# Moving the second exp, the weight sums and the casts of one unit in a fused attention and bilinear kernel

## The chip, the cores and the metric

The kernel runs on one core of a Trainium2 chip. A core has five engines with a queue each: TensorE (PE, matrix products), VectorE (DVE), ScalarE (ACT), GpSimd (POOL) and SyncE (SP), which here only issues transfers. The metric is the time of one execution on the device in microseconds (us), the median of several.

## What is computed

Chunked attention in chunks of 64 tokens, with its heads put side by side to 4608 tokens of 512 features, and behind it a bilinear layer of width 1536:

```python
batch, n_heads, seq, head_dim = (8, 8, 576, 64)
q_c = q.reshape(B, H, nc, chunk, D)            # chunk = 64, k_c and v_c likewise
scores = scale * np.matmul(q_c, k_c.transpose(0, 1, 2, 4, 3))
...
attn = np.exp(scores)
attn = attn / (np.sum(attn, axis=-1, keepdims=True) + 1e-09)
out = np.matmul(attn, v_c)
...
x = np.ascontiguousarray(attn_out.transpose(0, 2, 1, 3)).reshape(B * S, H * D)
a = x @ w_a
b = x @ w_b
return (a * b @ w_out).astype(np.float32)
```

The inputs and the output are float32 in the chip's memory. Inside, the attention is in bfloat16 and the bilinear layer in float16, with sums in PSUM in float32.

## The kernel before

**Tiling.** Attention goes in 18 units of 256 tokens, the bilinear layer in 9 blocks of 512 tokens, two units each. A unit is loaded (`load`, L181 and L193), cast to bfloat16 (`cast`, L212, mostly on POOL), transposed (units 0 to 4 on TensorE with copies on DVE and ACT, `transpose_pe`, L226 and L234; later ones by a transposing transfer, `transpose_dma`, L239), and then goes through `scores` (32 products, L257, and two exps on ACT, L266), `sums` (products with ones, L273, and logs, L283), `inverse` (exp of the negative log, L292) and `values` (32 products, L306, and two products with the inverse on DVE, L315, which make `xT`). `bring(U)` casts q and k of unit U, loads q of the next, transposes, casts v (`bring_v`) and loads k and v of the next.

**The bilinear layer.** Block 0 (`ab_step`, 12 steps `ft`) and block 1 (the same in 24 half steps, 256 tokens at a time: first the 12 steps for unit 2's tokens, then the 12 for unit 3's) use plain products: `x @ w_b` into PSUM (L368), a copy to SBUF by ACT (L376), `x @ w_a` and DVE's product of both (L377), which is `ab`. In half steps the PSUM banks alternate, pa and pq for `w_b`, pc and po for `w_a`. From block 2 on a form with seven products in place of eight is used (a Strassen variant). It needs sums of quarters of the weights (`combine_w`, L134, DVE: three parts and a fourth for each of six column pairs), of the tokens (`combine_x`, L398, DVE), of `w_out` (`combine_wo`, L163, POOL) and of `ab` (`combine_ab`, L498, POOL, four parts for each of three row pairs j). Its products are p1 to p7 of a `Group` (L418): p1 makes A, ACT copies A into B (L436), p6 adds to B, ACT copies that out as `u` (L429), p2 finishes A (`b_sb`), p5 adds to B and ACT copies it out as `v` (`v_sb`), p7 makes C. In the next step DVE adds v and u to C (`add7`, L456 and L457), p3 finishes B, p4 finishes C, and DVE multiplies (L468).

**The output product.** Block 0 uses `out_part` (L622, 12 products for each of four tiles in three parts) and a copy by ACT (L613). Later blocks use `OutGroup` (L554), also with seven products, which are dealt out in chunks of six matmuls between the products of the next block's steps (`chunks`).

**Order.** Nothing reorders the work: every engine runs its instructions in the order in which the program writes them. `at` puts the attention of the next block into fixed places (K, i, n) of the steps. In block 1 the order is written out by hand: `h(n)` does the next n half steps, and between them stand the scores, sums and values of units 3 to 5, `bring` of units 6 and 7 and block 0's output tiles. `combo()` writes the next of 18 weight sums. PSUM banks come from named pools of one bank each (pt has two, pb is two pools in turn), SBUF tiles from pools of fixed numbers of buffers.

Of the kernel before, what the change touches and what calls it, by code (L numbers as in the profile page):

```python
# [16 lines left out]
def kernel(  # L17
# [10 lines left out]
    nc = tc.nc  # L28
# [125 lines left out]
    def combine_wo(part, j):  # L154
        k = slice(2 * j, 2 * j + 2)
        k2 = slice(HFT + 2 * j, HFT + 2 * j + 2)
        b11, b12 = wo_sb[:, k, 0:256], wo_sb[:, k, 256:512]
        b21, b22 = wo_sb[:, k2, 0:256], wo_sb[:, k2, 256:512]
        t1, t2, t3, t4 = [t[:, k] for t in wo_t]
        o, x0, x1, op = (  # L160
            (t3, b22, b12, SUB), (t2, t3, b11, ADD), (t4, b21, t2, SUB), (t1, b12, b11, SUB)
        )[part]
        nc.gpsimd.tensor_tensor(out=o, in0=x0, in1=x1, op=op)  # L163
# [53 lines left out]
    def transpose_pe(U, names="qk"):  # L217
        if U not in qkt:
            qkt[U] = qkt_pool.tile([128, 2, 2, NKT, 128], BF16, name="qkt")
        for n in names:  # L220
            w = "qk".index(n)
            src = raw.pop((n, U))
            tp = bank().bitcast(BF16).rearrange("c (i m p) -> c i m p", i=2, m=NKT)
            for i in range(2):
                for m in range(NKT):
                    nc.tensor.transpose(  # L226
                        tp[:, i, m, :],
                        src[:, i, 2 * m:2 * m + 2, :].rearrange("p j d -> p (j d)"),
                        identity,
                    )  # L230
            dst = qkt[U][:, w].rearrange("c g m (p i) -> c i m g p", i=2)
            for i in range(2):
                cp = nc.vector.tensor_copy if w == 0 or U == 1 else nc.scalar.copy
                cp(out=dst[:, i], in_=tp[:, i].rearrange("c m (g p) -> c m g p", g=2))  # L234
# [10 lines left out]
    E_of = {}  # L245
    ln_of = {}
    rs_of = {}

    def scores(U, pools=(None, None)):
        t = qkt.pop(U)  # L250
        E_of[U] = sm_pool.tile([128, 2, NKT, 2, 64], BF16, name="E")
        sc = [bank(p).rearrange("p (m g s) -> p m g s", m=NKT, g=2) for p in pools]
        for m in range(NKT):
            for g in range(2):
                for j in range(2):
                    for cl in range(2):
                        nc.tensor.matmul(  # L257
                            sc[j][cl * 64:cl * 64 + 64, m, g, :],
                            t[j * 64:j * 64 + 64, 1, g, m, cl * 64:cl * 64 + 64],
                            t[j * 64:j * 64 + 64, 0, g, m, cl * 64:cl * 64 + 64],  # L260
                            start=m == 0 and g == 0,
                            stop=True,
                            skip_group_check=True,
                        )
        for j in range(2):
            nc.scalar.activation(out=E_of[U][:, j], in_=sc[j], func=AF.Exp, scale=scale)  # L266

    def sums(U, halves=None):
        E = E_of[U]
# [19 lines left out]
    def inverse(U, cl=None):  # L289

        for c in [slice(0, 2)] if cl is None else [cl]:
            nc.scalar.activation(  # L292
                out=rs_of[U][:, c], in_=ln_of[U][:, c], func=AF.Exp, scale=-1.0
            )

    def values(U):
        E, rs, vr = E_of.pop(U), rs_of.pop(U), raw.pop(("v", U))
        K, u = divmod(U, 2)
        if u == 0:
            x_tiles[K] = x_pool.tile([128, NKT, BLK], FP16, name="xT")  # L300
        av = [bank().rearrange("p (m g s) -> p m g s", m=NKT, g=2) for _ in range(2)]
        for m in range(NKT):
            for g in range(2):
                for cl in range(2):
                    for j in range(2):
                        nc.tensor.matmul(  # L306
                            av[cl][j * 64:j * 64 + 64, m, g, :],
                            vr[cl * 64:cl * 64 + 64, g, 2 * m + j, :],
                            E[cl * 64:cl * 64 + 64, j, m, g, :],
                            start=True,  # L310
                            stop=True,
                        )
        for cl in range(2):
            x = x_tiles[K][:, :, 256 * u:256 * u + 256]
            nc.vector.tensor_tensor(  # L315
                out=x.rearrange("p m (g c s) -> p m g c s", g=2, c=2)[:, :, :, cl, :],
                in0=av[cl],
                in1=rs[:, cl].rearrange("p m (g s) -> p m g s", g=2),
                op=MULT,
            )  # L320
# [13 lines left out]
    def bring(U, before_v=()):  # L334

        if U >= NU:
            return
        cast(U, "qk")
        load(U + 1, "q")
        transpose_dma(U)  # L340
        for args in before_v:
            cast(*args)
        bring_v(U)
# [288 lines left out]
    with tc.manual_schedule(  # L632
# [64 lines left out]

        for ft in range(NFT):
            ab_step(0, ft)
            if 3 <= ft < 10:  # L700
                combo()
            if ft == 6:
                transpose_pe(2)
            if ft == 8:
                slot(2)
            if ft == 9:
                sums(2)
                inverse(2)
            if ft == 10:
                values(2)  # L710

        cast(4, "qk")
        bring(5, [(4, "v")])

# [2 lines left out]
        def chunk(n=1):  # L717
            for _ in range(min(n, len(outs))):
                outs.pop(0)()

        def half(ft, u):
            ab_step(1, ft, 256 * u, 256 * u + 256)
            if ft > 9 if u == 0 else ft != 5 and ft != 9 and ft != 11:
                combo()
            if u == 1 and ft in (3, 5, 7):
                combine_w(ft // 2 - 1, 3)
            if u == 1 and ft % 2 and ft > 6:
                for part in range(3):
                    combine_ab(1, part, ft // 2 - 3)

# [2 lines left out]
        def h(n=1):  # L733
            for _ in range(n):
                half(*halves.pop(0))

        def normalize(U):
            sums(U)
            inverse(U)

        def out_0(tg):
            for p in range(3):
                out_part(0, tg, p, psum_b)
# [5 lines left out]
        h(3)  # L749
        scores(3)  # L750
        h(3)
        normalize(3)
        h(2)
        values(3)
        bring(6)
        h(8)
# [6 lines left out]
        normalize(4)  # L763
        h(1)
        scores(5)
        bring(7)
        h(1)
        values(4)
        h(1)
        spread[:] = [psum_q, psum_o]  # L770
        normalize(5)
        out_0(2)
        spread[:] = [psum_t]
        values(5)
        h(1)
        combine_x(2, (0, 1))
        whole = bank(psum_q)
        nc.tensor.matmul(whole, warm_in[:, :128], warm_in, start=True, stop=True)
        out_0(3)
        assert not halves and not combos  # L780

        attention = {}
# [29 lines left out]
        def attend(K, i, n):  # L812
# [2 lines left out]

        last = None
        chunks = {
            2: (0, 1, 1, 1, 1, 2, 1, 2, 1, 1, 2, 1),
            4: (1, 1, 1, 1, 2, 1, 1, 2, 2, 0, 1, 1),
            NBLK - 1: (1,) * 12,  # L820
        }
# [7 lines left out]

        for K in range(2, NBLK):  # L830
            for i in range(NWP):
                if K == 2 and i == 0:
                    for j in range(3):
                        combine_wo(3, j)
                if i == (2 if K == 2 else 1):
                    for j in range(3):
                        combine_ab(K - 1, 3, j)
                if i == 1:
                    bring(2 * K + 4)
                elif i == 3 and K > 2:  # L840
                    bring(2 * K + 5)
                elif i == 3:
                    cast(9, "qk")
                    load(10, "q")
                    transpose_dma(9)
                if i == 0:
                    g = OutGroup(K - 1)
                    outs += [
                        lambda g=g, n=n, th=th: g.part(n, th) for n in range(7) for th in range(2)
                    ]  # L850
                now = Group(K, i)
                now.p1()
                if last:
                    last.add7()
                chunk(chunks.get(K, chunks[4])[2 * i])
                if last:
                    last.p3()
                attend(K, i, 0)
                now.p6()
                if last:  # L860
                    last.p4()
                    finish(last)
                if K == 2 and i < 3:
                    combine_w(i + 3, 3)
                if K == 2 and i == 4:
                    bring_v(9)
                now.p2()
                chunk(chunks.get(K, chunks[4])[2 * i + 1])
                attend(K, i, 1)
                now.p5()  # L870
                now.p7()
                last = now
        ends = [
# [46 lines left out]
```

## Time and profile before

| | us |
|---|---|
| median of 5 runs | 309.06 |
| lowest and highest | 307.19, 311.4 |
| the profiled execution | 311.4 |
| its span, first to last instruction | 309.6 |

The profile is that of one execution; each of its views counts from the span's start. Its page says how busy each engine is and which chain of work ended last. TensorE's granted clock is full speed in all 40 slices. The 40 slices of the span, 7.7 us each, show TensorE's busy tenths, and the share of the 16 transfer engines, high up to about 108 us:

```profile
PE   2879999999997999998999999999999999999995
...
DMA  7999999999999999488929953995392001100025
```

How to read it: a line of the timeline has start and length in us, engine, line of the kernel, operation, what is written from what, shapes, and in brackets the idle time of the engine just before with what ended it. PE's rows overlap, since matmuls are pipelined; a stall is best read from the distance of starts: a matmul of 256 columns follows the last after 0.109 us, one of 512 after 0.217.

### The profile page before, as it was taken

The numbers are of one execution on the slowest core, as the hardware profiler recorded it, in microseconds if no ns is written. First come the engines' busy times: TensorE is split into PE (matmuls) and PEld (weight loads), VectorE is DVE, ScalarE is ACT, GpSimd is POOL, SyncE is SP. The second block draws the span as 40 slices with busy tenths as digits, with TensorE's granted clock in tenths as the row PEclk, the third lists the DMA queues.
The fourth block names the chain that finished last, engine by engine and source line by source line (L and its number), as shares of the span: only waits on it lengthen the run. The fifth ranks groups of instructions, "written<-read, shape, count | busy, mean of one in ns | idle before, by whom it ended". The sixth has DMA issues, their size and how long they took to land.

```text
span 309.6 us, 8537 instructions
## 1 busy us (share of the span) xinstructions
PE 291.5 (94%) x3497; PEld 231.6 (75%) x3499; DVE 213.1 (69%) x339; ACT 195.7 (63%) x353; POOL 192.7 (62%) x180
## 2 busy tenths in 40 slices
PE   2879999999997999998999999999999999999995
PEld 1534467765586888887888888888888888888884
DVE  3455673995757497578856885787678677965772
ACT  1643567348485658676768686768675877566531
POOL 0565758993859978915892588268727811780560
PEclk9999999999999999999999999999999999999999
DMA  7999999999999999488929953995392001100025
GB/s 229 307 382 265 265 314 338 214 208 203 211 245 248 201 206 281 81 201 185 257 57 238 234 162 70 209 263 146 78 227 97 11 2 70 51 20 2 1 80 193
DMA packets 143079, 54.56 MB, mean 176 GB/s; under 512 B 120256, under 2 KB 137152, under 8 KB 143040
## 3 DMA queue, kind: packets, MB, share of 16 engines
q1 hardware_dynamic: 142896, 53.88, 69.4%
q8 instruction: 27, 0.44, 0.6%
q10 hardware_dynamic: 144, 0.13, 0.1%
q14 instruction: 12, 0.10, 0.1%
HBM read 37.75 MB, written 9.44 MB: 152 GB/s over the span
## 4 chain that ended last, share of the span: by engine, by line
PE 59%; DMA 17%; POOL 9%; SPq 6%; DVE 5%; ACT 2%; issue 1%; POOLq 0%; DVEq 0%
PE pb L418 15%; PE pc L418 11%; PE pa L418 10%; PE po L554 10%; PE pq L554 9%; DMA st<-in_moe_w_a_dram 5%; DMA st<-in_v_dram 5%; SPq L181 4%; DMA st<-in_moe_w_out_dram 3%; POOL wot L163 2%; DMA st<-in_moe_w_b_dram 2%; POOL so L498 2%; DMA st<-in_k_dram 2%; SPq L193 2%; ACT E L266 1%
## 5 line engine op out<-in xcount | busy, mean ns | idle before, releaser
L418 PEld LDWEIGHTS <-t 128*128 128x128 f16 x504 | 48.3, 98 | 11.6 <-issue 5.9
L498 POOL TENSOR_TENSOR so<-ab_sb 128x512 f16<-128x512 f16 x23 | 26.5, 1154 | 45.2 <-DVE ab_sb L468 45.2
L456 DVE TENSOR_TENSOR c_sb<-pc,v_sb 128x512 f32<-128x512 f32 x42 | 29.0, 689 | 32.6 <-ACT v_sb L429 31.5
L418 PE MATMUL pb<-s,wa 128*128 128x256 f16 x336 | 50.6, 273 | 0.0
L418 PE MATMUL pa<-xT,wb 128*128 128x256 f16 x336 | 50.4, 273 | 0.0
L554 PEld LDWEIGHTS <-ab_sb 128*128 128x128 f16 x384 | 37.6, 98 | 4.7 <-issue 0.4
L418 PEld LDWEIGHTS <-wb 128*128 128x128 f16 x336 | 32.9, 98 | 4.0
L429 ACT COPY u_sb<-pb 128x512 f32<-128x512 f32 x42 | 24.7, 588 | 16.8 <-PE pb L418 11.6
L418 PEld LDWEIGHTS <-wa 128*128 128x128 f16 x336 | 31.7, 98 | 4.3 <-issue 0.2
L212 POOL CAST k_raw<-st 128x1024 bf16<-128x1024 f32 x17 | 18.2, 1068 | 26.3 <-DMA st<-in_k_dram 26.3
L468 DVE SCALAR_TENSOR_TENSOR ab_sb<-pb,b_sb 128x512 f16<-128x512 f32 x42 | 28.9, 688 | 7.6 <-PE pb L418 7.0
L468 DVE SCALAR_TENSOR_TENSOR ab_sb<-pc,c_sb 128x512 f16<-128x512 f32 x42 | 28.9, 688 | 5.6 <-PE pc L418 4.7
L554 PEld LDWEIGHTS <-so 128*128 128x128 f16 x288 | 28.0, 98 | 5.7 <-issue 1.2
L429 ACT COPY b_sb<-pa 128x512 f32<-128x512 f32 x42 | 25.0, 595 | 8.5 <-PE pa L418 7.3
L436 ACT COPY pb<-pa 128x512 f32<-128x512 f32 x42 | 24.5, 583 | 9.0 <-PE pa L418 9.0
L457 DVE TENSOR_TENSOR pc<-pc,u_sb 128x512 f32<-128x512 f32 x42 | 29.0, 689 | 0.0
L212 POOL CAST v_raw<-st 128x1024 bf16<-128x1024 f32 x18 | 19.2, 1064 | 14.7 <-DMA st<-in_v_dram 5.8
L498 POOL TENSOR_TENSOR so<-so,ab_sb 128x512 f16<-128x512 f16 x23 | 26.7, 1160 | 1.8
L429 ACT COPY v_sb<-pb 128x512 f32<-128x512 f32 x42 | 24.7, 587 | 4.8 <-PE pb L418 4.7
L498 POOL TENSOR_TENSOR ab_sb<-ab_sb 128x512 f16<-128x512 f16 x23 | 26.9, 1169 | 0.0
L418 PE MATMUL pc<-s,t 128*128 128x256 f16 x168 | 25.2, 272 | 1.1 <-DVE ab_sb L468 1.1
L498 POOL TENSOR_TENSOR so<-ab_sb,so 128x512 f16<-128x512 f16 x23 | 26.1, 1161 | 0.0
(130 smaller groups left out, 579.3 us busy)
## 6 DMA issues: line engine op xcount, KB each, us to landing
out_dram<-o_sb SPq DMA_DIRECT2D x34, 256.0 KB, 3.3
st<-in_v_dram SPq DMA_DIRECT2D x32, 256.0 KB, 5.1
st<-in_q_dram SPq DMA_DIRECT2D x25, 256.0 KB, 4.9
st<-in_k_dram SPq DMA_DIRECT2D x25, 256.0 KB, 3.5
st<-in_moe_w_b_dram SPq DMA_DIRECT2D x6, 512.0 KB, 7.7
st<-in_moe_w_a_dram SPq DMA_DIRECT2D x6, 512.0 KB, 7.9
st<-in_moe_w_out_dram SPq DMA_DIRECT2D x6, 512.0 KB, 7.0
st<-in_q_dram SPq DMA_DIRECT2D x3, 512.0 KB, 5.9
```

The source lines that it names most:

```text
L163: nc.gpsimd.tensor_tensor(out=o, in0=x0, in1=x1, op=op)
L181: nc.sync.dma_start(out=st[p:p + n, g], in_=src[b, :, s:s + n, :].rearrange("h p d -> p h d"))
L193: nc.sync.dma_start(out=st[r // 2:(r + m) // 2].rearrange("p h i d -> p h (i d)"), in_=src[b, :, s:s + m, :].rearrange("h (p i) d -> p h ( ...
L212: eng.tensor_copy(out=raw[n, U], in_=staged.pop((n, U)))
L418: nc.tensor.matmul(t[:, h * 256:h * 256 + 256], w[:, kt, h * 128:h * 128 + 128], x[:, kt], start=start and h == 0 and kt == 0, stop=h == 1 ...
L429: nc.scalar.copy(out=t, in_=src)
L436: nc.scalar.copy(out=self.B, in_=self.A)
L456: nc.vector.tensor_tensor(out=self.c, in0=self.C, in1=self.v, op=ADD)
L457: nc.vector.tensor_tensor(out=self.C, in0=self.C, in1=self.u, op=ADD)
L468: nc.vector.scalar_tensor_tensor(out=self.dst[:, :, c0:c0 + 256], in0=t.rearrange("p (h n) -> p h n", h=2), scalar=AB_SCALE, in1=o.rearran ...
L498: (eng or nc.gpsimd).tensor_tensor(out=o, in0=x0, in1=x1, op=op)
L554: nc.tensor.matmul(t[:, c0:c0 + 256], a[:, kt, th * 128:th * 128 + 128], w[:, kt], start=n in (0, 4) and first and kt == 0, stop=last and ...
```

## The change

Five things are moved; nothing is computed differently, and one instruction is added (an inverse in two halves).

1. `scores` writes its exps into a list. The second one, where the scores stand beside a group's products with banks of their own (units 7 and 9 to 17, ten times), is written behind p5 and its copy; elsewhere both are written at once as before.
2. Weight sums (`combo`) start at block 0's second step in place of its fourth, and lie in half steps 2, 4, 6 of the first half and in the even steps of the second; before they lay in steps 10 and 11 of the first half and in nine of the second.
3. Block 0's transposes of unit 2 are split: q behind step 6, k behind step 7. The inverse of unit 3 is written in two halves with a half step between.
4. Unit 7's casts (q, k, v on POOL) are laid between the sums of ab of block 1 for row pair 1, which stood behind all three casts.
5. Block 0's output: the first part of tile 2 stands before the sums of unit 5, and the third part of tile 3 behind p1 of block 2's first step, with `combine_wo`'s fourth part behind it.

```diff
+    late = []
+
     def scores(U, pools=(None, None)):
...
+        E = E_of[U]
         for j in range(2):
-            nc.scalar.activation(out=E_of[U][:, j], in_=sc[j], func=AF.Exp, scale=scale)
+            late.append(
+                lambda j=j: nc.scalar.activation(
+                    out=E[:, j], in_=sc[j], func=AF.Exp, scale=scale
+                )
+            )
+        exps(1 if pools[0] else 2)
+
+    def exps(n=2):
+        while late and n:
+            late.pop(0)()
+            n -= 1
...
             ab_step(0, ft)
-            if 3 <= ft < 10:
+            if 1 <= ft < 10:
                 combo()
-            if ft == 6:
-                transpose_pe(2)
+            if ft in (6, 7):
+                transpose_pe(2, "qk"[ft - 6])
...
             ab_step(1, ft, 256 * u, 256 * u + 256)
-            if ft > 9 if u == 0 else ft != 5 and ft != 9 and ft != 11:
+            if ft in ((2, 4, 6), (0, 2, 4, 6, 8, 10))[u]:
                 combo()
...
-            if u == 1 and ft % 2 and ft > 6:
+            if u == 1 and ft in (7, 11):
                 for part in range(3):
                     combine_ab(1, part, ft // 2 - 3)
...
-        normalize(3)
-        h(2)
+        sums(3)
+        inverse(3, 0)
+        h(1)
+        inverse(3, 1)
+        h(1)
         values(3)
...
         scores(5)
-        bring(7)
+        cast(7, "q")
         h(1)
+        combine_ab(1, 0, 1)
+        cast(7, "k")
+        load(8, "q")
+        transpose_dma(7)
+        combine_ab(1, 1, 1)
+        combine_ab(1, 2, 1)
+        bring_v(7)
         values(4)
         h(1)
         spread[:] = [psum_q, psum_o]
+        out_part(0, 2, 0, psum_b)
         normalize(5)
-        out_0(2)
+        out_part(0, 2, 1, psum_b)
+        out_part(0, 2, 2, psum_b)
...
-        out_0(3)
+        for p in range(2):
+            out_part(0, 3, p, psum_b)
+        outs.append(lambda: out_part(0, 3, 2, psum_b))
...
-            2: (0, 1, 1, 1, 1, 2, 1, 2, 1, 1, 2, 1),
+            2: (1, 1, 1, 1, 1, 2, 1, 2, 1, 1, 2, 1),
...
-                if K == 2 and i == 0:
-                    for j in range(3):
-                        combine_wo(3, j)
...
                 chunk(chunks.get(K, chunks[4])[2 * i])
+                if K == 2 and i == 0:
+                    for j in range(3):
+                        combine_wo(3, j)
...
                 now.p5()
+                exps()
                 now.p7()
```

## The prediction, made before the changed kernel ran

> **What bounds the kernel now.** I read the page first (busy shares, then the chain that ended last), then that chain in order of time, the waits of TensorE, and the timeline of each engine in the stretches where TensorE waits.
>
> TensorE is busy for 94% of the span, so there is little to win: 18 us of idle, 5.5 of them before its first instruction.
>
> ```profile
> PE 291.5 (94%) x3497; PEld 231.6 (75%) x3499; DVE 213.1 (69%) x339; ACT 195.7 (63%) x353; POOL 192.7 (62%) x180
> ...
> PE 59%; DMA 17%; POOL 9%; SPq 6%; DVE 5%; ACT 2%; issue 1%; POOLq 0%; DVEq 0%
> ```
>
> The chain in order of time (start, us, what) shows where that matters. Up to 100.8 us it runs through SP, transfers and POOL, and TensorE is not on it; from 101.98 us it is TensorE, with short visits to ACT and DVE.
>
> ```profile
> 83.70 5.40 DMA st<-in_v_dram
> 89.24 1.04 POOL v_raw L212
> 90.28 1.12 POOL so L498
> ...
> 97.40 3.38 POOL wo L163 x3
> 101.98 0.54 PE pb L418 x4
> ```
>
> So a wait that TensorE loses before 72 us is worth nothing by itself: what comes next there is a transfer. The waits of TensorE after 26 us (us in total, times, longest) name the two that the POOL chain makes:
>
> ```profile
> PE pq L554 <- POOL wo L163: 0.9, 2, 0.7
> PE pq L554 <- POOL so L498: 0.9, 1, 0.9
> PE pt L226 <- POOL k_raw L212: 0.8, 1, 0.8
> PE pb L418 <- ACT pb L436: 0.4, 1, 0.4
> ```
>
> And the stretch before the POOL chain's end, POOL alone, the last brackets being its idle time and what ended it:
>
> ```profile
> 83.73 1.23 POOL L212 CAST q_raw<-st 128x1024 bf16<-128x1024 f32 x1
> 85.67 1.04 POOL L212 CAST k_raw<-st 128x1024 bf16<-128x1024 f32 x1 [0.71 <-DMA st<-in_k_dram]
> 89.24 1.04 POOL L212 CAST v_raw<-st 128x1024 bf16<-128x1024 f32 x1 [2.53 <-DMA st<-in_v_dram]
> ```
>
> POOL stands idle for 0.71 + 2.53 us here while three sums of ab (pair 1, L498) that need no transfer are queued behind the cast of unit 7's values.
>
> **The change part by part.** The instruction orders of the two kernels, side by side, show that SP's order is the same, that POOL's differs only here, and that ScalarE has one instruction more.
>
> *Unit 7's casts between the sums.* The order becomes q, sum, k, sum, sum, v, three sums, then the three w_out sums of L163. With the rows' durations: q starts at 83.73 as before (the cast of unit 6's values at 79.04 waits for a transfer and is not touched), a sum 84.96 to 86.1, k to 87.1, two sums to 89.45, v (landed by 89.24) to 90.45, three sums of 1.16 to 93.9, L163 3.37 to 97.3 instead of 100.77: 3.4 us earlier. What TensorE lost to it is read from starts (a 256-column matmul follows the last by 0.109 us): 96.20 - (94.73 + 0.44) = 1.03; 99.71 - (99.17 + 0.22) = 0.32; 100.83 - (99.71 + 0.22) = 0.90; together 2.25 us. It would reach those points at 95.2, 98.35 and 98.6 without waiting; the operands are now ready at 92.8, 96.2 and 97.3. All 2.25 go, with 1.3 to spare. What is queued behind: k's cast ends 0.4 to 0.7 us later, and behind it SP's transpose of k, which SP only reaches at 91.25; no cost up to 3.9 us of delay. The load of q(8) and the loads of k(8), v(8) keep their places on SP. Next in line on POOL are unit 8's casts: v(8) is issued at 93.86 and 95.27, and v loads land 5.3 us after issue (median of this stretch), so at 100.6; then come the three sums of the fourth kind, done at 105.1, where TensorE wants them from 105.4 to 105.9. Covered by about 0.5 us.
>
> *Third part of the last out tile behind p1, and one part of out tile 2 before the sums of unit 5.* No work is added. ScalarE now copies A to B (L436) before the out tile's copy (L613), so p6 at 84.46, which waited 0.36 us for L436, is free: gain 0.4. The sums of unit 5 waited 0.24 us for a bank at 75.85, now beside 0.87 us of out tile: gain 0.25. Together 0.65, before the POOL chain's waits. With the slack of 1.3 above, both sums add. L163's sums now stand behind the last part of out tile 3 as well, but TensorE is through with that near 83.2, ten us before POOL gets there.
>
> *Second exp behind p5's copy.* Ten steps. Where the step after has no chunk to spare (steps 4 of blocks 3 to 6), ScalarE's two exps (0.49 us each by their starts) hold up v_sb, then DVE's two adds, then p4:
>
> ```profile
> 172.64 0.59 ACT L266 ACTIVATE E<-pb 128x512 bf16<-128x512 f32 x1
> 173.12 0.59 ACT L429 COPY v_sb<-pb 128x512 f32<-128x512 f32 x1
> 173.74 0.69 DVE L456 TENSOR_TENSOR c_sb<-pc,v_sb 128x512 f32<-128x512 f32 x1 [0.63 <-ACT v_sb L429]
> 174.35 0.69 DVE L457 TENSOR_TENSOR pc<-pc,u_sb 128x512 f32<-128x512 f32 x1
> 175.09 0.60 PE L418 MATMUL pc<-xT,t 128*128 128x256 f16 x4
> ```
>
> p4 could start at 174.41 + 0.44 = 174.85: 0.24 us lost, and the same at 143.88, 205.28, 235.48. Block 7 has no scores there and shows the new order: v_sb 0.65 us after p5's start, p4 (265.15) unhindered. So p5 at 172.00 gives v_sb at 172.65, the adds end 0.46 us earlier and 0.24 is gained in blocks 4 to 6. What is late next is p7, which needs DVE's product of C: with the sums of x (L398) it would allow p7 at 176.78, TensorE arrives at 176.83. In block 3 this is already the limit: p7 at 146.86 waited 1.02 us, because L398 took 1.42 us beside POOL's sum; there I take 0.15. Sum 3 x 0.24 + 0.15 = 0.87. The other six steps show no wait at p4: nothing. The moved exp ends where v_sb ended, the next L436 starts when it did (173.58).
>
> *Weight sums, transposes and the split inverse before 72 us.* Moving k's transposes one step removes 0.76 us of waiting at 32.27; thinning the sums in the half steps removes DVE's hold-ups at 56.04, 58.90, 60.20 and 61.38 (0.11 + 0.24 + 0.42 + 0.31 = 1.08 us, by starts); the split inverse lets c_sb through 0.5 us earlier at 53.32, but DVE's xT follows as before, so 0 to 0.29. Up to 2.1 us, and I book none: the scores of unit 5 at 72.63 already wait 0.3 us for the transposed k,
>
> ```profile
> L239 SPq DMA_TRANSPOSE qkt<-k_raw x2: 1242/1414/1587, 69.6 to 79.7; - x2
> ...
>   DMA qkt<-k_raw: 0.3, 1
> ```
>
> whose issue at 69.59 follows SP's loads, and the loads fill the transfer engines (share 1.09 from 47 to 63 us, 0.89 from 63 to 73). TensorE will come early and wait. If the transfers came earlier too, up to 2 us would be added; bounds 0 and -2.1, value 0, as SP's order is the same.
>
> Here a rule speaks against the change. Row first: a weight sum (L134, 128x512) takes 0.41 us alone, 0.73 to 0.87 on average before 102 us and at most 1.37. The Trainium skill, "SBUF — State Buffer", section "Who interferes with whom", says that a VectorE instruction with two SBUF inputs contends with a GpSimd one that reads SBUF, and that the later of the two is blocked until the other is through. Taken at its worst (a whole cast of 1.04, then 0.41) a sum costs 1.45 us, and two half steps with one sum 2 x 0.41 + 1.45 = 2.27 us of DVE against 1.75 of TensorE: six pairs would lose up to 3 us. By the row, 0.82 + 0.87 = 1.69, it fits. I take the row; by the rule the early 2.1 us would turn into a loss of about 1 us by 72.6. The sums of block 0's steps 1 and 2 have 1.73 us a step: covered by either.
>
> *The sum.* 2.25 + 0.65 + 0.87 = 3.8 us. The profiled execution took 311.4 us (309.6 of span, 1.8 around it): 307.6. It is the slowest of five, 2.3 us over the median; if the quicker runs have transfers that come up to 2.3 us earlier, TensorE's early gains come through by as much as the POOL wait shrinks, so most of the 3.8 stays (I take off 0.1). On the median: 309.06 - 3.7 = 305.4 us.
>
> **The rivals.** *Given back to the transfers.* POOL ends its chain earlier and then waits for v(8), and SP's transfers are near their limit to 112 us (share 0.98 from 83.7 to 112.8). For: the cover is only 0.5 us. Against: the transposes of unit 8 may now be issued at 99.9, when SP gets there, rather than 101.78. If v(8) lands 2 us later than I think, 1.5 of the 2.25 us are lost: 306.9.
>
> *Early gains come through.* If the transposed k(5) lands earlier with the rest of the loads, up to 2 us more: 303.4. Against: no transfer is moved.
>
> *Slower: ScalarE idles for p5.* v_sb now stands before an exp that could run at once. If p5's result comes later than the first exp's end, ScalarE idles, the exp and the next copy A to B (L436) are late, and p6 waits. Point of decision: L436 ends at about 173.58 + 0.62 = 174.20 and p6 is at 174.41, so more than 0.2 us. At 0.7 us it would cost 0.5 in ten steps, 5 us, and the 0.87 would not come: 305.4 + 5.9 = 311.3. Against: exp one ends at 172.63 and p5's result is there at 172.65.
>
> That the change doesn't do what it says is excluded by the instruction orders for ten pairs of exp and copy, and for POOL.
>
> **How the numbers follow.** Forecast 0.52 (own range 304.2 to 306.4), given back 0.28 (305.9 to 308.4), early gains 0.11 (302.5 to 304.2), slower 0.09 (309 to 313). About 1% is what a measurement of this kernel can tell from no change, 305.97 here. Faster by over 1%: 0.43 of the forecast, 0.01 of the second, 0.11 of the third, 0.55. Slower by over 1% (from 312.15) takes the upper part of the last case and unknown waits, 0.06. Within 1%: 0.39. The range, 303.3 to 308.2, leaves out the slower case and the ends of the two others.
>
> **What would show it.** Right: no wait of L554 on POOL near 93 to 98 us; v_sb ahead of the second exp and no gap before p4 in blocks 4 to 6; the scores of unit 5 still at about 72.6 us, waiting 1 to 2 us for the transposed k. Wrong: the start of block 2's second step unmoved, a wait of L554 on the fourth sums near 105, p6 waiting for L436 after the exps, or weight sums of over 1 us holding TensorE in the half steps.

## The result, and the profile after

| | before | after |
|---|---|---|
| median | 308.32 (77 runs) | 306.71 (40 runs) |
| lowest and highest | 306.68, 311.4 | 304.72, 310.62 |
| profiled execution | 311.4 | 307.22 |
| its span | 309.6 | 305.4 |

All in us. The ratio is 0.9946 (95% interval 0.9932 to 0.9959): 1.7 us faster, where 3.7 were forecast. The execution that was profiled before the change is the slowest of all 77, so it stands for the slow end of that kernel and not for its median. The two profiled executions differ by 4.2, close to the 3.8 of the sum; on the median less than half of the sum is left. The rest of this document finds out why.

The page after, busy times and the chain that ended last:

```profile
PE 289.8 (95%) x3497; PEld 231.3 (76%) x3499; DVE 213.9 (70%) x339; ACT 196.3 (64%) x354; POOL 192.4 (63%) x180
...
PE 70%; DMA 15%; DVE 5%; POOL 3%; SPq 3%; issue 2%; ACT 0%; POOLq 0%; DVEq 0%
```

POOL fell from 9% of the chain to 3%. POOL's order in the changed kernel (lines of the code are 13 higher there: L511 are the sums of ab that were L498):

```profile
82.69 1.23 POOL L212 CAST q_raw<-st 128x1024 bf16<-128x1024 f32 x1
83.88 1.33 POOL L511 TENSOR_TENSOR so<-ab_sb 128x512 f16<-128x512 f16 x1
85.16 1.24 POOL L212 CAST k_raw<-st 128x1024 bf16<-128x1024 f32 x1
...
88.57 1.03 POOL L212 CAST v_raw<-st 128x1024 bf16<-128x1024 f32 x1
...
93.20 3.56 POOL L163 TENSOR_TENSOR wo<-wo 128x512 f16<-128x512 f16 x3
```

There is no idle time in it, and L163 ends at 96.8, 4.0 us earlier than in the first profile of before. TensorE's waits (us in total, times, longest) name two others in place of POOL:

```profile
PE pc L431 <- DVE ab_sb L481: 1.5, 3, 0.9
PE pt L259 <- DMA qkt<-k_raw: 0.9, 1, 0.9
```

The second is at the scores of unit 5, at 71.89 us: TensorE comes early and waits for the transposed k, as forecast. The first is p7, which waits for DVE's product of C. One of its places was not forecast, the first step of block 3:

```profile
114.65 1.16 POOL L511 TENSOR_TENSOR so<-so,ab_sb 128x512 f16<-128x512 f16 x1
114.89 1.20 DVE L411 TENSOR_TENSOR s<-xT 128x512 f16<-128x512 f16 x1
...
115.76 1.34 POOL L511 TENSOR_TENSOR ab_sb<-ab_sb 128x512 f16<-128x512 f16 x1
...
116.01 1.37 DVE L411 TENSOR_TENSOR s<-xT,s 128x512 f16<-128x512 f16 x1
...
117.30 0.68 DVE L481 SCALAR_TENSOR_TENSOR ab_sb<-pc,c_sb 128x512 f16<-128x512 f32 x1
...
118.03 0.60 PE L431 MATMUL pc<-s,t 128*128 128x256 f16 x4 [0.94 <-DVE ab_sb L481]
```

Two sums of x (0.41 us each when alone) take 1.20 and 1.37 beside POOL's sums, DVE's product comes late, and p7 starts 1.1 us late. In the first profile of before the same sums, at 118.56 and 119.40, took 0.91 and 0.41 and no wait followed. A like collision stood elsewhere in that profile, though, in the last step of block 3, where p7 was 1.0 us late:

```profile
144.31 1.16 POOL L498 TENSOR_TENSOR ab_sb<-ab_sb 128x512 f16<-128x512 f16 x1
144.33 1.42 DVE L398 TENSOR_TENSOR s<-xT 128x512 f16<-128x512 f16 x1
```

### The profile page after: what moved, and what is told of

The parts are those of the page before. It is cut to its first block, busy times and chain, and to the rows that moved or that the text cites. A ratio compares the mean times of both kernels' runs of the same rounds, so it can differ in the third digit from the quotient of the medians.

```text
span 305.4 us, 8539 instructions
## 1 busy us (share of the span) xinstructions
PE 289.8 (95%) x3497; PEld 231.3 (76%) x3499; DVE 213.9 (70%) x339; ACT 196.3 (64%) x354; POOL 192.4 (63%) x180
## 4 chain that ended last, share of the span: by engine, by line
PE 70%; DMA 15%; DVE 5%; POOL 3%; SPq 3%; issue 2%; ACT 0%; POOLq 0%; DVEq 0%
PE pb L431 18%; PE pc L431 12%; PE pa L431 11%; PE po L567 11%; PE pq L567 9%; DMA st<-in_moe_w_a_dram 5%; DMA st<-in_k_dram 3%; DMA st<-in_q_dram 2%; DVE s L411 2%; DMA st<-in_moe_w_b_dram 2%; PE pb L635 2%; PE pt L319 2%; SPq L181 2%; POOL wot L163 2%; DMA st<-in_moe_w_out_dram 2%
## 5 line engine op out<-in xcount | busy, mean ns | idle before, releaser
L511 POOL TENSOR_TENSOR so<-ab_sb 128x512 f16<-128x512 f16 x23 | 26.9, 1169 | 42.7 <-DVE ab_sb L481 42.7
L567 PEld LDWEIGHTS <-ab_sb 128*128 128x128 f16 x384 | 37.6, 98 | 4.7 <-issue 0.4
L567 PEld LDWEIGHTS <-so 128*128 128x128 f16 x288 | 28.1, 98 | 3.4
L511 POOL TENSOR_TENSOR so<-so,ab_sb 128x512 f16<-128x512 f16 x23 | 26.7, 1160 | 1.7
L511 POOL TENSOR_TENSOR ab_sb<-ab_sb 128x512 f16<-128x512 f16 x23 | 27.1, 1180 | 0.0
L511 POOL TENSOR_TENSOR so<-ab_sb,so 128x512 f16<-128x512 f16 x23 | 26.1, 1163 | 0.0
```

Of the source, the lines that this page charges most:

```text
L511: (eng or nc.gpsimd).tensor_tensor(out=o, in0=x0, in1=x1, op=op)
L567: nc.tensor.matmul(t[:, c0:c0 + 256], a[:, kt, th * 128:th * 128 + 128], w[:, kt], start=n in (0, 4) and first and kt == 0, stop=last and ...
```

## The experiments

Theory A: the first profile had late transfers, and POOL's 2.25 us are rarely there. Theory B: part of the gain is given back at p7. Theory C came up after the first four kernels, theory D with the last four. Each ratio is to the kernel before on the same chip, with its 95% interval.

**The kernel before once more.**

> The kernel before, unchanged, for a second profile of it. Theory A (the sum was made from an execution with late transfers): its span is nearer to 306.5 than to 309.6 us, and the waits of L554 on POOL near 96 to 101 us are clearly below the 2.25 us of the first profile, 1 us or less. Theory B (the gain is given back after 105 us): the waits on POOL are there as in the first profile, 2 us or more.

It took 307.81 us, span 306.0. POOL's timeline there:

```profile
83.11 1.31 POOL L212 CAST k_raw<-st 128x1024 bf16<-128x1024 f32 x1 [0.54 <-DMA st<-in_k_dram]
85.31 1.04 POOL L212 CAST v_raw<-st 128x1024 bf16<-128x1024 f32 x1 [0.88 <-DMA st<-in_v_dram]
...
93.31 3.56 POOL L163 TENSOR_TENSOR wo<-wo 128x512 f16<-128x512 f16 x3
```

v of unit 7 is cast at 85.31, 3.9 us earlier than in the first profile, and TensorE has no wait for POOL at all there, though L163 ends as late as in the changed kernel's first profile (96.87 and 96.76). This execution is close to the median of its kernel on that chip (307.96). Theory A holds so far: the 2.25 us are not in every execution. A third profile of the same stretch comes with e2 below.

**One part at a time.** Unit 7's casts between the sums alone:

```diff
-            if u == 1 and ft % 2 and ft > 6:
+            if u == 1 and ft in (7, 11):
...
-        bring(7)
-        h(1)
+        cast(7, "q")
+        h(1)
+        combine_ab(1, 0, 1)
+        cast(7, "k")
...
+        bring_v(7)
```

> Unit 7's casts between the sums of ab, alone. Forecast of the prediction: 2.25 us less (ratio 0.993). Theory A: the waits on POOL that are typically there go and no more, about 1 us less (0.996 to 0.998). Theory B: in its profile the waits of L554 on POOL are gone, but L398 in block 2's last step and block 3's first takes 1.2 us or more beside POOL's sums and p7 waits 0.4 and 1.1 us there, where the kernel before has 0.2 and 0; the net is then nearly nothing (0.998 to 1.000).

0.9996 (0.9971 to 1.002). L163 ends at 93.8, 3 us before e0's, and TensorE is where it was (the sums in block 2's fourth step at 98.5 and 98.7). No L554 waits on POOL. p7 is 0.73 us late at 143.62, in block 3's last step and not in its first; as the kernel before had 1.0 us there in its first profile, this is no sign of B.

The second exp alone:

```diff
+        exps(1 if pools[0] else 2)
...
                 now.p5()
+                exps()
                 now.p7()
```

> The second exp behind p5's copy, alone. Forecast: 0.24 us of p4's wait gone in each of blocks 3 to 6, 0.87 us in all (ratio 0.997). If ScalarE idles for p5 (the slower rival), p6 waits for L436 after scores and the time rises by up to 5 us.

0.9974 (0.9954 to 0.9994), 0.8 us: as forecast. No p4 wait is left in blocks 3 to 6, and ScalarE does not idle between the two exps.

Up to 96 us this kernel has the order of the kernel before, so its profile is a third sample of the POOL wait. Its execution took 309.36 us, one of the slower ones (its median is 307.24):

```profile
88.30 1.04 POOL L212 CAST v_raw<-st 128x1024 bf16<-128x1024 f32 x1 [2.03 <-DMA st<-in_v_dram]
```

TensorE's waits for POOL:

```profile
PE pq L567 <- POOL wo L163: 0.9, 2, 0.7
...
PE pq L567 <- POOL so L511: 0.5, 1, 0.5
```

By starts that is 1.9 us in three places (0.69, 0.32 and 0.89). So the wait was no accident of one execution: it comes with a late v, in two executions from the slow end, and is absent in the one near the median. How many executions have it cannot be told from three profiles.

The weight sums, transposes and the split inverse alone:

```diff
-            if 3 <= ft < 10:
+            if 1 <= ft < 10:
...
-            if ft == 6:
-                transpose_pe(2)
+            if ft in (6, 7):
+                transpose_pe(2, "qk"[ft - 6])
...
-            if ft > 9 if u == 0 else ft != 5 and ft != 9 and ft != 11:
+            if ft in ((2, 4, 6), (0, 2, 4, 6, 8, 10))[u]:
...
-        normalize(3)
-        h(2)
+        sums(3)
+        inverse(3, 0)
+        h(1)
+        inverse(3, 1)
+        h(1)
```

> Weight sums, split transposes and split inverse, alone: all of it before 72 us. Forecast: no gain (ratio 1.000, 0.998 to 1.002), TensorE comes to the scores of unit 5 up to 2 us earlier and waits there about as much for the transposed k. If early gains come through: 1 to 2 us less (0.993 to 0.997).

0.9992 (0.997 to 1.0014): nothing, as forecast. In its profile the scores of unit 5 start at 70.85, 1.0 us before e0's, and the waits show both places where the early start is lost, 0.5 us by starts at the transposed k and 1.9 at POOL:

```profile
PE pq L554 <- POOL wo L163: 0.9, 2, 0.7
...
PE pq L554 <- POOL so L498: 0.5, 1, 0.5
...
PE pt L257 <- DMA qkt<-k_raw: 0.4, 1, 0.4
```

These three give 0.4% together, and the whole 0.54%. The intervals are wide enough to hide that gap; if it is real, either the output tiles (not run alone) carry the rest, or parts need each other: theory C, that TensorE's early arrival and POOL's order hide each other's worth.

**Combinations.** POOL's order and the early edits, without the exps and the output tiles:

> Unit 7's casts between the sums of ab and all of the edits before 72 us together (each alone gave nothing). Theory C (the two limits hide each other: with the early edits alone TensorE comes 1.5 us sooner to the products that wait for POOL and waits there, with POOL's order alone POOL is sooner but TensorE is not): together they gain more than the sum of both, 0.8 to 1.5 us (ratio 0.995 to 0.9975), and its profile has no wait of L554 on POOL near 93 to 98 us. Against it: the ratio is the product of the two, 0.999, as the gain is given back at p7 in blocks 2 and 3.

0.9984 (0.9964 to 1.0004). No wait on POOL, as C says, but the gain is not clear of nothing. p7 waits 0.96 at 112.12 (block 2's last step) and 0.52 at 142.98, by starts; the first is 0.8 more than e0 has there.

All but unit 7's casts:

> The whole change but for unit 7's casts, which stay as before. Theory C: only the exps' 0.8 us remain (ratio 0.997), and TensorE waits about 2 us or more for POOL near 93 to 98 us. If the casts' place is worth nothing: 0.9946, the ratio of the whole change.

0.9974 (0.9953 to 0.9996), the exps' share and no more. TensorE's waits:

```profile
PE pq L567 <- POOL wo L163: 0.9, 2, 0.7
...
PE pq L567 <- POOL so L511: 0.3, 1, 0.3
```

v of unit 7 is cast at 85.84 here, half a microsecond after e0's, where TensorE waited for nothing. The difference is TensorE: its p6 of block 2's first step starts at 81.57 in place of 83.82. It comes earlier, and loses 1.7 us (by starts) to POOL. So with timely transfers the casts' place is worth something only beside what makes TensorE early; in executions with late ones (the first profile and e2's) the waits say that it would be worth something alone. The intervals of this kernel and of the whole change overlap, so the medians don't show that the casts' place is needed; the waits of this one profile carry the reading.

All but the edits before 72 us:

> The whole change but for the edits before 72 us (weight sums, split transposes, split inverse as before). Prediction as written (no early gain is booked): the same as the whole change, 0.9946. Theory C (both limits must move): the early edits carry about 1 us of the whole, so 0.997 to 0.998, and the casts' place brings little here, as TensorE is not early enough to wait for POOL.

0.9944 (0.9916 to 0.9971), the same as the whole within about 0.3%. C's forecast for these edits (0.997 to 0.998) is not met: on the median they carry nothing that was measured, as the prediction booked, though up to 0.8 us is not excluded. In this profile p6 of block 2's first step starts at 82.36, 1.5 us before e0's, without them: so the output tiles are what can make TensorE early here.

**The changed kernel again.**

> The changed kernel again, on the same chip as the two above and the next: ratio 0.993 to 0.996. In the profile, p7's waits for DVE in blocks 2 and 3 are between 0.4 and 1.5 us in sum, depending on where POOL's sums fall.

0.9947 (0.9926 to 0.9968). This profiled execution took 305.1 us and had early transfers, like e0. So the two can be set side by side, stage by stage. The stretches end at the scores of unit 5, at p6 of block 2's first step, of its fourth step, of block 3, of block 4 and of block 8, and at the end of the span. The first number after a stretch is its length, then come each engine's busy time and number of instructions. e0, before:

```profile
core 0: us, PE busy (x) PEld busy (x) DVE busy (x) ACT busy (x) POOL busy (x), PEclk, DMA share, GB/s
0.00:71.80 71.80, 62.07 (x684) 38.76 (x686) 44.03 (x74) 35.86 (x68) 49.13 (x50) 1.00 1.04 285
71.80:83.80 12.00, 11.44 (x186) 6.60 (x186) 9.15 (x17) 7.34 (x15) 7.34 (x8) 1.00 1.04 218
83.80:99.00 15.20, 15.12 (x194) 12.51 (x193) 10.91 (x15) 12.10 (x22) 14.16 (x14) 1.00 1.05 252
...
115.20:145.50 30.30, 30.13 (x393) 25.77 (x390) 22.23 (x36) 22.20 (x39) 19.61 (x19) 1.00 0.80 190
145.50:265.60 120.10, 119.68 (x1520) 102.83 (x1517) 88.76 (x140) 87.88 (x154) 71.99 (x66) 1.00 0.55 132
```

e6, after:

```profile
0.00:70.40 70.40, 61.16 (x684) 38.46 (x686) 42.87 (x75) 35.81 (x69) 48.06 (x50) 1.00 1.04 288
70.40:81.30 10.90, 10.88 (x186) 6.28 (x185) 7.57 (x13) 6.92 (x14) 7.43 (x8) 1.00 1.05 228
81.30:96.60 15.30, 15.16 (x207) 12.52 (x194) 12.68 (x18) 12.45 (x23) 15.22 (x15) 1.00 1.06 255
...
112.80:143.60 30.80, 30.16 (x393) 25.84 (x390) 23.32 (x36) 22.33 (x39) 19.62 (x20) 1.00 0.82 187
143.60:262.90 119.30, 119.30 (x1520) 102.89 (x1517) 89.19 (x140) 88.28 (x154) 71.99 (x66) 1.00 0.57 136
```

The lengths in all four profiles of the two kernels, by the same starts:

| stretch up to | before | after | e0, before | e6, after |
|---|---|---|---|---|
| scores of unit 5 | 72.6 | 71.9 | 71.8 | 70.4 |
| p6, block 2, first step | 11.8 | 10.9 | 12.0 | 10.9 |
| p6, block 2, fourth step | 17.5 | 15.3 | 15.2 | 15.3 |
| p6, block 3 | 16.2 | 16.4 | 16.2 | 16.2 |
| p6, block 4 | 31.2 | 31.3 | 30.3 | 30.8 |
| p6, block 8 | 120.0 | 119.2 | 120.2 | 119.3 |
| end | 40.4 | 40.4 | 40.4 | 40.4 |

In the first pair, with late transfers, the stretch with the POOL waits gives 2.2 us, close to the 2.25 that was booked; in the second, with early transfers, it gives nothing. The output tiles' stretch gives about 1 in both, and blocks 4 to 7, where only the exps differ, 0.7 and 0.8. The edits before 72 us give 1.4 in the second pair. That gain is not in every profile: five profiles with these edits (e3, e4, e5, e6 and e11) have the scores at 70.4 to 70.9, and three (after, e7, e10) at 71.5 to 72.2, after waits of 1.0 to 1.6 us by starts for the transposed k; e8, without the edits, has them at 71.45.

Block 3 is 0.5 longer in e6 than in e0. Its rows show why. e0:

```profile
140.31 1.16 POOL L498 TENSOR_TENSOR ab_sb<-ab_sb 128x512 f16<-128x512 f16 x1
...
140.93 0.68 DVE L468 SCALAR_TENSOR_TENSOR ab_sb<-pb,b_sb 128x512 f16<-128x512 f32 x1
141.08 0.60 PE L418 MATMUL pc<-xT,t 128*128 128x256 f16 x4 [0.17 <-DVE pc L457]
...
141.53 0.42 DVE L398 TENSOR_TENSOR s<-xT 128x512 f16<-128x512 f16 x1
```

e6:

```profile
138.42 0.60 PE L431 MATMUL pc<-xT,t 128*128 128x256 f16 x4
138.63 1.16 POOL L511 TENSOR_TENSOR ab_sb<-ab_sb 128x512 f16<-128x512 f16 x1
138.79 1.28 DVE L411 TENSOR_TENSOR s<-xT 128x512 f16<-128x512 f16 x1
...
141.18 0.38 PE L431 MATMUL pc<-s,t 128*128 128x256 f16 x2 [0.64 <-DVE ab_sb L481]
```

In e0 p4 (pc<-xT,t) came 0.33 us late by starts and DVE's sum of x then began just as POOL's third sum ended. In e6 p4 is on time, DVE's sum starts while POOL's third sum has most of its time left and takes 1.28 in place of 0.42; p7 is 0.8 us late. That this is the moved exp's doing is not shown. The same collision stands in the kernel before (144.33 above) and in e1, where p4 is late as well, and block 3 took 30.3 to 31.2 us in the five profiles without the moved exp (before, e0, e1, e3, e4) and 30.4 to 31.3 in the five of after, e2, e5, e6 and e8.

**Towards a version that beats both.** The sums of x out from between DVE's products at the block's start:

```diff
-                attention[K, 0, 0] = [lambda K=K: combine_x(K, (2, 3))]
+                attention[K, 0, 1] = [lambda K=K: combine_x(K, (3,))]
...
+            at(K, 5, 1, lambda u: combine_x(u // 2, (2,)), U + 1)
```

> The changed kernel with the third sum of x (L411) written half a step before the block and the fourth half a step later, so that neither stands between DVE's two products of a step. Theory B (part of the gain is given back there): p7's waits of block 3 on go, about 1 us less than the changed kernel (ratio 0.990 to 0.993). If those waits cost nothing, or only move to p4 behind the next add7: the same as the changed kernel, 0.9946.

0.9921 (0.9893 to 0.995; 306.22 us beside 307.1 for the changed kernel on that chip). In its profile the waits at p7 in blocks 3 and 8's first steps are gone, and p4 in block 8's first waits 0.32 instead; those in the last steps of blocks 2 and 3 stay (0.75 and 0.76 by starts), where the two sums of x stand that were not moved. The direction is B's, but the intervals of the two kernels overlap, so a gain over the changed kernel is not shown.

Unit 5's transposes ahead of the loads of q(6):

```diff
-        bring(5, [(4, "v")])
+        cast(5, "qk")
+        transpose_dma(5)
+        load(6, "q")
+        cast(4, "v")
+        bring_v(5)
```

> The changed kernel with unit 5's transposing transfers ahead of the loads of q(6) on SP. Theory D (transfers are what takes back a part of the early gains, at unit 5's scores): the scores of unit 5 wait for nothing in its profile, and the time is 0.3 to 1 us less than the changed kernel (ratio 0.991 to 0.9935). If the wait only moves on, because SP now waits about 1.5 us for the cast of k and all loads behind it are late: the same or slower than the changed kernel, 0.9946 to 0.998.

0.9917 (0.9885 to 0.9949). The profile is that of an execution of 307.67 us: the scores of unit 5 start at 70.63 without a wait, and the wait has moved on to unit 6's scores and to POOL:

```profile
PE pt L259 <- DMA qkt<-k_raw: 1.0, 1, 1.0
...
PE pq L567 <- POOL wo L163: 0.5, 1, 0.5
```

Both outcomes that were written down are in it: the median is 0.9 us lower than the changed kernel's ratio would make it, with overlapping intervals, and the profile shows the delay passed on. Whether it helps stays open.

Unit 11's values cast one step later, in the changed kernel and in the one with the sums of x spread:

```diff
-                elif i == 3 and K > 2:
+                elif i == 3 and K > 3:
                     bring(2 * K + 5)
...
-                if K == 2 and i == 4:
-                    bring_v(9)
+                if K < 4 and i == 4:
+                    bring_v(2 * K + 5)
```

> The changed kernel with the cast of unit 11's values one step later, behind the first three sums of ab in block 3 (in block 2 unit 9's already stands so). Theory B: p7's wait for DVE in block 3's last step, 0.2 to 0.8 us in the profiles of the changed kernel, is gone, since POOL's sums are through before L411 starts: 0.3 to 0.8 us less than the changed kernel (0.992 to 0.9935). If that wait comes from elsewhere: 0.9946.

> The same cast moved in the kernel with the sums of x spread out (0.9921): 0.9895 to 0.991 if both waits at p7 are real and separate, 0.992 if they are not.

0.9956 (0.9934 to 0.9977) and 0.9898 (0.9862 to 0.9935, of six runs, median 305.67). The first is a miss: p7 in block 3's last step still waits, 0.84 and 0.82 us by starts. In the second kernel the moved cast itself has taken the sum's place:

```profile
138.96 1.32 DVE L411 TENSOR_TENSOR s<-xT 128x512 f16<-128x512 f16 x1
138.96 1.04 POOL L212 CAST v_raw<-st 128x1024 bf16<-128x1024 f32 x1
```

So this profile gives the cast no part in the step from 0.9921 to 0.9898. The kernel has the lowest median here, from few runs; that it beats e7 is not shown.

## Why the prediction was right or wrong

**The direction, the range and two of the terms were right.** The exps were put at 0.87 us and measured alone at 0.8 (blocks 4 to 7 are 0.7 to 0.8 shorter in both pairs of profiles). The edits before 72 us were booked at nothing: alone 0.9992, and left out of the whole 0.9944 against 0.9946. The reason given, the wait for the transposed k, is only a part of it. It showed as forecast in the first profile of the changed kernel (1.03 us by starts); where the scores did come early, the gain was lost later in e3 and e5, at POOL (1.9 and 1.7 us), and in e4 in part at p7, and was kept in e6. Between like profiles L163 ends 2.7 to 4.0 us earlier (e0 and e6, the two first ones), and no product of L567 waits for POOL in the two profiles of the changed kernel.

**The step that failed is the last of the sum**, "so most of the 3.8 stays (I take off 0.1)", which carried the POOL term of 2.25 us from the profiled execution to the median. The wait is 2.25 us in that execution, the slowest, 1.9 in e2's, also from the slow end, and 0 in e0's, near the median, where v of unit 7 is cast 3.9 us earlier; and the casts' place alone is worth 0.04%, within 0.3%. The argument was that in quicker runs TensorE's early gains come through by as much as the wait shrinks. They do between e0 and e6 (1.4 us), but on the median they are worth nothing that was measured (e8). The bound of the term from below should have been 0, which one execution, the slowest of five, could not exclude. The case called "given back to the transfers" had the size of the loss about right, 306.9, and that is luck: its place is not where the loss is, as v(8) is cast at 99.0 with 0.27 us of waiting, and no wait on the fourth sums is seen.

**What took its place.** The output tiles, put at 0.65, measured 1.1 (stage two of e0 and e6). From the last product ahead of the sums of unit 5 to the next half step e0 takes 4.59 us and e6 3.95 with the same work, so 0.64 came there, where 0.25 was booked; from that half step to p6 it is 5.22 and 4.78, so 0.44, where 0.4 was. They start TensorE earlier into the stretch where POOL's order then matters: without it (e5) the whole is worth the exps' 0.26%, with it 0.54%. So I read the 1.7 us on the median as the exps and the output tiles, with POOL's order as the condition of the second rather than a gain by itself. This is argued and not shown: the intervals of e5 and of the whole overlap, and the output tiles were not run alone, so that they give nothing without POOL's order is untested on the median.

**A term that was missing: p7.** The prediction had p7 as what is late next after the exps, with 0.05 us of margin in blocks 4 to 6 and a gain of 0.15 left in block 3. The margin held. In block 3 the waits move from profile to profile in both kernels, by up to 1 us, so that neither the 0.15 nor a loss can be told there. A loss that goes with the change stands one place earlier, at p7 in block 2's last step: 0.17 or 0.18 us by starts in the six profiles of before, e0, e1, e2, e3 and e8, and 0.23 to 0.97 in all eight others, which have the early edits together with POOL's order, the output tiles or both. In e4 DVE's two sums of x take 1.09 and 1.26 us beside POOL's sums there. This may be where a part of the early gains goes; no run here takes it away by itself.

**The rule that was weighed** (the Trainium skill, "SBUF — State Buffer", "Who interferes with whom") was right in kind. At the weight sums its worst case, a loss of 1 us by 72.6, did not come: e6 has the scores 1.4 us earlier than e0. At the sums of x, of which the prediction had one row (1.42 us) and did not ask the rule, the delay is what blocking would make: 1.2 to 1.4 us in place of 0.42, each sum ending about 0.3 us after a POOL instruction did.

**The slower rival** did not come: in e6's block 4 the copy of v starts 0.76 us after p5 (166.31 and 167.07), and p6 is 0.08 late (168.81 after 168.29 + 0.44).

## What to carry to other kernels

A wait that a transfer makes in one profile is a sample: take a second profile before pricing it, and set its lower bound to zero if it was in the slowest run. Where two engines run near each other's limit, an edit on one of them can measure as nothing alone; look at where the wait goes in its profile, and try the pair. Before a wait in the changed kernel is called the change's doing, look for it in more than one profile of the kernel before: here block 3 alone differed by 0.9 us between two profiles of the same program.

## What I had not expected of the hardware

The landing of the same transfer moved by almost 4 us between executions of one kernel: v of unit 7 was cast, at once on landing by the trace, at 89.24 and at 85.31 us, while the span up to the scores of unit 5 moved by 0.8 only. Most of it is not the transfer itself: SP issued these loads from 82.54 us in the one and from 79.85 in the other, and unit 5's transposes already from 68.15 and 65.88. Why SP's queue was behind is not shown. And DVE's sums of x beside POOL took 1.20 to 1.42 us in both first profiles, e6 and e11, of which 0.41 is their own time.
